# The last chunk's second product as 26 block products (4x4 by 4x2) in place of 28 (two times 2x2 by 2x2)

## The chip, the core and the metric

The kernel runs on one core of one Trainium2 chip. The metric is the device time of one launch in microseconds. Before the change it is 485.75 us, the median of 3 runs (485.72 to 485.87). The profile is of one execution, whose span is 485.1 us at a granted TensorE clock of 1.00; times "at 451.78" are microseconds from the start of that span.

## What is computed

A gated linear attention with a matrix state (mLSTM) is followed by a feed-forward block. Only the second is touched by the change:

```python
# x: (3072, 320), w_in: (320, 2048), w_out: (2048, 320), all float32
h = x @ w_in
g = h * (1.0 / (1.0 + np.exp(-1.702 * h)))
return (g @ w_out).astype(np.float32)
```

The kernel takes the sequence of 768 steps in six chunks of 128 (`w` = 0 to 5, `NW` = 6), for 4 batches and 8 heads. A chunk gives 4 blocks of 128 tokens, one for each batch, so for a chunk the first product is (512 x 320) by (320 x 2048) and the second (512 x 2048) by (2048 x 320). While the second product of chunk `w` runs, the attention of chunk `w+1` is woven between its parts. Chunk 5 has no successor: behind its first product there is only its second product and the stores.

## The kernel before: the parts that matter

Both products of chunks 1 to 5 are done in float32 with Strassen's scheme in Winograd's form: a 2x2 by 2x2 product of blocks takes 7 block products instead of 8, and sums of blocks of both factors have to be made for it. The order of the instructions on each engine is the order of the program.

The first product, one call for each half of the 2048 columns (`j` = 0 and `j` = 4), each over four pairs of column tiles `k`:

```python
def up_fast(w, j, between=None):
    ...
    if j == 0:                       # sums of the tokens' side, on VectorE (L506 to L509)
        V.tensor_tensor(out=bt1, in0=b01, in1=b00, op=OP.subtract)
        ...
    if between:
        between()                    # chunks 1 to 4, j == 0: work for the next chunk
    ...
    product(chain, 0, a00, b00, True)    # L518, TensorE
    take(0, 0)                           # L523, ScalarE: copy from PSUM
    product(other, 0, a01, b10, True)
    product(chain, 0, as2, bt2)
    take(0, 1)
    product(other, 1, as4, b11)
    product(chain, 0, a10, b01)
    take(1, 1)
    product(chain, 1, as1, bt1)
    for k in js:
        add(k, 0, 1, chain, 1)           # L526, VectorE: g = PSUM + g
    for k in js:
        for i, p in enumerate((other, chain)):
            r = slice(i * 64, i * 64 + 64)
            T.matmul(p[k], w_in_x[r, k, :], x[r, 2, :], start=False, stop=True, skip_group_check=True)  # L546
    for k in js:
        add(k, 1, 1, chain, 1)
        add(k, 0, 0, other, 0)
        gelu(k, 0, 0)                    # L530, ScalarE
    product(chain, 0, a11, bt4)
    for k in js:
        gelu(k, 1, 0, chain[k][:, ts[0]])
    for k in js:
        add(k, 0, 1, other, 1)
        gelu(k, 0, 1)
    for k in js:
        gelu(k, 1, 1)
```

The matmul at L546 on `chain[k]` writes the bank that `add(k, 0, 1, chain, 1)` has to read first, so it waits for that addition.

The second product, one call for each pair of batches `c`; each of its 7 products is 8 matmuls with 128x128 stationary and 160 moving columns:

```python
def product(a, b, *adds):
    po = ps_m.tile([128, DH], FP, tag="m", name="p_out")          # DH = 160
    for f in range(NH):                                           # NH = 8
        T.matmul(po, a(f), b[:, f, :], start=(f == 0), stop=(f == NH - 1))    # L615
    for dst, x in adds:
        if x is None:
            V.tensor_copy(out=dst, in_=po)                        # L618
        else:
            V.tensor_tensor(out=dst, in0=x, in1=po, op=OP.add)    # L620
```

The sums of `w_out` that it needs (`t1`, `t2`, `t4`, and `w01` in place) are made once in chunks 0 and 1 on VectorE (`weight_sums`, L585). The sums of the hidden values (`hidden_sums`, L596) are made in each chunk on VectorE, partly between the halves of the first product, partly beside the second.

Of the kernel before, what the change touches and what calls it, by code (L numbers as in the profile page):

```python
# [8 lines left out]
FP = mybir.dt.float32  # L9
U32 = mybir.dt.uint32  # L10
BF = mybir.dt.bfloat16
AF = mybir.ActivationFunctionType
OP = mybir.AluOpType
# [9 lines left out]
L = 128  # L23
# [11 lines left out]
def kernel(  # L35
# [12 lines left out]
    nc = tc.nc  # L48
    B, H, S, D = q.shape
    BH = B * H  # L50
    DM = H * D
    DFF = moe_w_in.shape[1]
    NW = S // L
    NP = H // 2
    NF = DFF // 128
    D1 = D + 1
    DP = 64
    W = B * L
    NH = NF // 2
    DH = DM // 2  # L60
# [5 lines left out]
    work = ctx.enter_context(tc.tile_pool(name="work", bufs=2))  # L66
    gp = ctx.enter_context(tc.tile_pool(name="gp", bufs=NH))
    op = ctx.enter_context(tc.tile_pool(name="op", bufs=2))
    rows = ctx.enter_context(tc.tile_pool(name="rows", bufs=2, space=bass.MemoryType.DRAM))
    ps_a = ctx.enter_context(tc.tile_pool(name="ps_a", bufs=4, space=PSUM))  # L70
    ps_m = ctx.enter_context(tc.tile_pool(name="ps_m", bufs=2, space=PSUM))
    ps_x = ctx.enter_context(tc.tile_pool(name="ps_x", bufs=2, space=PSUM))
    ctx.enter_context(tc.manual_schedule())

    V, A, G, T = nc.vector, nc.scalar, nc.gpsimd, nc.tensor
# [8 lines left out]
    k_st = const.tile([L, BH, DP], FP, name="k_st")  # L84
# [502 lines left out]
    def hidden_sums(w, c, js, *what):  # L587

        for j in js:
            s1, s2, s4 = (total(i, c)[:, 2 * j:2 * j + 2, :] for i in range(3))  # L590
            h00, h10, h01, h11 = (gs[w, k * 4 + j][:, :, (2 * c + two) * L:(2 * c + two + 1) * L]
                                  for k in range(2) for two in range(2))
            for x in what:
                out_, in0, in1, f = {1: (s1, h10, h11, OP.add), 2: (s2, s1, h00, OP.subtract),
                                     3: (h10, h00, h10, OP.subtract), 4: (s4, h01, s2, OP.subtract)}[x]
                V.tensor_tensor(out=out_, in0=in0, in1=in1, op=f)  # L596
# [5 lines left out]
    def down_fast(w, c):  # L602
        o = [op.tile([128, DM], FP, tag="o", name="o_sb") for _ in range(2)]
        o00, o01, o10, o11 = (o[i][:, n * DH:(n + 1) * DH] for i in range(2) for n in range(2))

        def block(two, k):
            return lambda f: gs[w, k * 4 + f // 2][:, f % 2, (2 * c + two) * L:(2 * c + two + 1) * L]

        def summed(i):
            return lambda f: total(i, c)[:, f, :]  # L610

        def product(a, b, *adds):
            po = ps_m.tile([128, DH], FP, tag="m", name="p_out")
            for f in range(NH):
# [4 lines that stand above are left out]
                else:  # L619
                    V.tensor_tensor(out=dst, in0=x, in1=po, op=OP.add)  # L620

        last = w == NW - 1 and c == 1

        def store(two, cols=slice(0, DM)):
            b = 2 * c + two
            nc.sync.dma_start(out=out[b * S + w * L:b * S + (w + 1) * L, cols], in_=o[two][:, cols])

        def left_done():

            if last:  # L630
                store(0, slice(0, DH))

        return [lambda: product(block(0, 0), w00, (o00, None), (o01, None)),
                lambda: (product(block(0, 1), w10, (o00, o00)), left_done()),
                lambda: product(summed(1), t2, (o01, o01)),
                lambda: product(block(1, 0), w01, (o10, o01)),
                lambda: product(summed(0), t1, (o11, o10), (o01, o01)),
                lambda: (product(block(1, 1), t4, (o10, o10)), store(1)),
                lambda: (product(summed(2), w11, (o01, o01)), store(0, slice(DH if last else 0, DM)))]

    def attention(w):
        if w > 1:

            return [[(columns, w)], [(weights, w, 0), (weights, w, 1)],
                    [(scores, w, 0), (hidden_sums, w - 1, 1, range(4), 3), (scores, w, 1), (weights, w, 2),
                     (weights, w, 3)],
                    [(values, w, 0), (values, w, 1), (scores, w, 2), (scores, w, 3)] +  # L650
                    [(scale, w, b) for b in (0, 1) if w + 1 < NW],
                    [(seam, w, 0), (seam, w, 1), (last_values, w)], [(carry, w)] if w + 1 < NW else [],
                    [(seam, w, 2)], [(seam, w, 3)]]
        return [[(columns, w)], [(weights, w, 0), (weights, w, 1)], [(scores, w, 0), (scores, w, 1)],
                [(weights, w, 2), (gates_out, w), (values, w, 0, 1), (scale, w, 0), (scale, w, 1)],
                [(weights, w, 3), (scores, w, 2), (scores, w, 3)], [(seam, w, 0), (seam, w, 1)],
                [(last_values, w)], [(seam, w, 2), (seam, w, 3)], [(new_states, w), (carry, w)]]
# [96 lines left out]
    def next_keys():  # L754
# [3 lines left out]
        transposes(w + 1, 0)  # L758
        transposes(w + 1, 1)

    for w in range(NW):
        more = w + 1 < NW
        for j in range(NF // 2):
            if w == 0 and j == 0:
                for pair_ in range(2):
                    for i, g in enumerate(hidden_of(0, pair_)):
                        A.activation(out=g, in_=first[pair_][i], func=AF.Gelu_apprx_sigmoid)
                    if pair_ == 0:
                        weights_in(0)
            elif w == 0 and j % 2 == 0:  # L770
                weights_in(j // 2)
                up(j, j == 2)
            elif w and j % 4 == 0:
                up_fast(w, j, next_keys if more and j == 0 else None)
            if w == 0 and j == 0:
                load_blocks(1, 0)
                spread(1)
                load_blocks(1, 1)
            if w == 1 and j == 3:
                weight_sums(3)  # L780
            if more:
                if w and j == 0:
                    load(w + 1, "o")
                if j == 4:
                    load(w + 1, "v")
                    if w:
                        spread(w + 1)
                    else:
                        fetch(17)
                        load(1, "o")  # L790
                if j == (4 if w else 6):
                    load(w + 1, "k")
                if w and j == 3:
                    for b in range(2, 4):
                        transposes(w + 1, b)
            if w and j in (3, 7):
                hidden_sums(w, 0, (j // 4 * 2, j // 4 * 2 + 1), 1, 2)
                if j == 3:
                    hidden_sums(w, 0, (0, 1), 3, 4)
        side = attention(w + 1) if more else []  # L800
        if w == 0:

            blocks = [(lambda b=b, n=n: down(w, b, n)) for ns in ((0, 1), (2,), (3,)) for b in range(B) for n in ns]
            stops = (0, 1, 5, 6, 8, 10, 12, 14, 15)
        else:
            blocks = down_fast(w, 0) + down_fast(w, 1)
            stops = (0, 1, 2, 4, 8, 10, 11, 12)
        for i, block in enumerate(blocks):
            if w == 0:
                weights_in(4 + i)  # L810
                if i == 0:
                    load_gates(2)
                if i == 2:
                    for b in range(B):
                        transposes(1, b, slice(0, 1))
                    first_sums((0, 1))
                    for b in range(B):
                        transposes(1, b, slice(1, 2))
                if i == 10:
                    load_blocks(2)  # L820
            elif w + 2 < NW and i == 0:
                load_gates(w + 2)
                load_blocks(w + 2)
            block()
            if i in stops and side:
                run(side.pop(0))
            if w == 1 and i == 1:
                weight_sums(2)
            if w:
                for at, c, *what in ((0, 0, (2, 3), 3), (1, 0, (2, 3), 4), (1, 1, range(4), 1),  # L830
                                     (5, 1, range(2), 2), (6, 1, range(2, 4), 2), (7, 1, range(4), 4)):
                    if i == at:
                        hidden_sums(w, c, *what)
                if i == 2 and not more:
                    hidden_sums(w, 1, range(4), 3)
            elif i == 11:
                weight_sums(0)
                weight_sums(1)
# [30 lines left out]
```

## Time and profile before

| what | value |
|---|---|
| device time, median of 3 | 485.75 us |
| span of the profiled run | 485.1 us |
| last chunk, first product, first half | 419.69 to 435.65 us |
| last chunk, first product, second half | 435.65 to 451.78 us |
| last chunk, second product (112 matmuls of the program) | 451.78 to 482.22 us |
| last addition and last store | 482.25 to 485.1 us |

The second product stands with x224 in the profile, because a float32 matmul of the program leaves two records there. The records' lengths overlap, so the mean of 301 ns beside L615 is not what one costs; the time from the start of one group to the start of the next is. The same holds on VectorE and GpSimd: an operation's duration includes the end of its pipeline, and the next one starts some 0.04 to 0.08 us before that end.

### The profile page before, as it was taken

How to read it: one execution, taken by the hardware profiler on the slowest of the kernel's cores; microseconds unless marked ns; L12 is line 12 of the kernel's file. 1: busy time of each engine (PE TensorE's matmuls, PEld its weight loads, DVE VectorE, ACT ScalarE, POOL GpSimd, SP SyncE). 2: the span in 40 equal slices, each digit the busy share in tenths (PEclk: the TensorE clock that was granted, in tenths of full speed). 3: DMA queues.
4: the chain of work that ended last, by engine and by line, in shares of the span. 5: the costliest groups of instructions: out<-in, count | busy, mean ns of one | idle time of the engine just before them, and what ended most of it. 6: DMA issues, size and time to landing. Idle time of an engine off the chain costs nothing. (4 is left out here: it accounts for less than half of the span.)

```text
span 485.1 us, 10434 instructions
## 1 busy us (share of the span) xinstructions
PE 479.3 (99%) x4072; PEld 397.8 (82%) x4072; DVE 343.0 (71%) x853; ACT 220.6 (45%) x575; POOL 60.4 (12%) x101
## 2 busy tenths in 40 slices
PE   8999999999999999999999999999999999999997
PEld 5874466777779999787999877999977999977997
DVE  8788887987978965667766677696576786254831
ACT  6767672603549302467600465900374920255300
POOL 3020001430000430000331000332000120000000
PEclk9999999999999999999999999999999999999999
DMA  9999689964996100997000896300492000000000
GB/s 126 197 262 286 112 208 191 170 85 71 153 215 73 14 28 30 188 178 82 4 29 9 122 249 70 32 28 3 79 262 26 1 15 16 28 1 0 1 34 22
DMA packets 176098, 44.87 MB, mean 92 GB/s; under 512 B 164369, under 2 KB 169649, under 8 KB 176049
## 3 DMA queue, kind: packets, MB, share of 16 engines
q1 hardware_dynamic: 175472, 43.55, 49.1%
q8 instruction: 32, 0.52, 0.4%
q10 hardware_dynamic: 576, 0.66, 0.4%
q14 instruction: 18, 0.14, 0.1%
HBM read 40.17 MB, written 4.01 MB: 91 GB/s over the span
## 5 line engine op out<-in xcount | busy, mean ns | idle before, releaser
L615 PE MATMUL p_out<-w_out_sb,g 128*128 128x160 f32 x480 | 69.8, 301 | 0.0
L615 PEld LDWEIGHTS p_out<-w_out_sb,g 128*128 128x128 f32 x480 | 66.3, 190 | 0.9
L405 ACT COPY xT<-p_x 128x384 f32<-128x384 f32 x24 | 10.8, 482 | 120.5 <-PE p_x L404 107.3
L526 DVE TENSOR_TENSOR g<-p_u,g 128x256 f32<-128x256 f32 x80 | 33.7, 424 | 44.6 <-PE p_u L518 35.0
L523 ACT COPY g<-p_u 128x256 f32<-128x256 f32 x120 | 43.0, 376 | 43.5 <-PE p_u L518 39.3
L530 ACT ACTIVATE g<-g 128x256 f32<-128x256 f32 x120 | 42.3, 423 | 39.3 <-DVE g L526 39.3
L336 POOL TENSOR_SCALAR_AFFINE_SELECT wt<-wt 128x1024 f32<-128x1024 f32 x20 | 22.7, 1136 | 240.9 <-ACT wt L334 201.9
L620 DVE TENSOR_TENSOR o_sb<-o_sb,p_out 128x160 f32<-128x160 f32 x70 | 21.4, 317 | 42.2 <-PE p_out L615 41.8
L334 ACT ACTIVATE wt<-wt,cols 128x128 f32<-128x128 f32 x160 | 47.9, 394 | 0.0
L518 PE MATMUL p_u<-xT,w_in_sb 128*128 128x256 f32 x160 | 38.9, 382 | 0.0
L518 PE MATMUL p_u<-xs,big 128*128 128x256 f32 x160 | 37.8, 379 | 0.0
L546 PE MATMUL p_u<-xT,w_in_x 64*128 64x512 f32 x80 | 37.0, 602 | 0.0
L546 PE MATMUL p_v<-xT,w_in_x 64*128 64x512 f32 x80 | 37.0, 602 | 0.0
L566 PE MATMUL p_out<-w_out_sb,g 128*128 128x320 f32 x128 | 36.4, 437 | 0.0
L352 DVE TENSOR_TENSOR wt<-p_s,wt 128x512 f32<-128x512 f32 x48 | 30.4, 682 | 8.2 <-POOL wt L336 6.7
L615 PE MATMUL p_out<-t,big 128*128 128x160 f32 x240 | 35.5, 301 | 0.0
L518 PEld LDWEIGHTS p_u<-xT,w_in_sb 128*128 128x128 f32 x160 | 29.6, 190 | 5.4 <-DVE o_sb L620 1.5
L518 PEld LDWEIGHTS p_u<-xs,big 128*128 128x128 f32 x160 | 30.0, 190 | 4.6
L615 PEld LDWEIGHTS p_out<-t,big 128*128 128x128 f32 x240 | 33.3, 190 | 0.2
L566 PEld LDWEIGHTS p_out<-w_out_sb,g 128*128 128x128 f32 x128 | 23.7, 190 | 10.0 <-issue 0.5
L526 DVE TENSOR_TENSOR g<-p_v,g 128x256 f32<-128x256 f32 x80 | 29.8, 414 | 0.0
L546 PEld LDWEIGHTS p_v<-xT,w_in_x 64*128 64x128 f32 x80 | 14.2, 186 | 16.0 <-issue 16.0
(172 smaller groups left out, 859.8 us busy)
## 6 DMA issues: line engine op xcount, KB each, us to landing
wt<-m_row SPq DMA_DIRECT2D x20, 512.0 KB, 6.9
v_st<-in_v_dram SPq DMA_DIRECT2D x5, 640.0 KB, 8.8
eo<-in_o_gate_dram SPq DMA_DIRECT2D x5, 640.0 KB, 5.6
k_st<-in_k_dram SPq DMA_DIRECT2D x5, 640.0 KB, 11.4
out_dram<-o_sb SPq DMA_DIRECT2D x19, 160.0 KB, 1.8
big<-in_moe_w_in_dram SPq DMA_DIRECT2D x5, 512.0 KB, 7.1
k_bl<-in_k_dram SPq DMA_DIRECT2D x40, 64.0 KB, 2.9
q_bl<-in_q_dram SPq DMA_DIRECT2D x40, 64.0 KB, 2.8
```

The lines of the kernel that those rows point to most:

```text
L334: A.activation(out=x[:, h, :], in_=x[:, h, :], func=AF.Exp, scale=-1.0, bias=cols[w][:, b * H + h:b * H + h + 1])
L336: G.affine_select(out=x, in_=x, compare_op=OP.is_ge, fill=0.0, base=0, pattern=[[0, H], [1, L]], channel_multiplier=-1)
L352: V.tensor_tensor(out=wt[w, b][:, :, i, :], in0=pw[i], in1=wt[w, b][:, :, i, :], op=OP.mult)
L405: A.copy(out=xT[w][:, :, b, :], in_=px)
L518: T.matmul(p[k][:, ts[t]], a[:, k // 2, k % 2 * 128:(k % 2 + 1) * 128], b, start=first, stop=True, skip_group_check=True)
L523: A.copy(out=g[k][i][:, ts[t]], in_=chain[k][:, ts[0]])
L526: V.tensor_tensor(out=g[k][i][:, ts[t]], in0=p[k][:, ts[pt]], in1=g[k][i][:, ts[t]], op=OP.add)
L530: A.activation(out=dst, in_=dst if src is None else src, func=AF.Gelu_apprx_sigmoid)
L546: T.matmul(p[k], w_in_x[r, k, :], x[r, 2, :], start=False, stop=True, skip_group_check=True)
L566: T.matmul(po, gs[w, f // 2][:, f % 2, b * L:(b + 1) * L], w_out_sb[:, f, :], start=(f == 0), stop=(f == NF - 1))
L615: T.matmul(po, a(f), b[:, f, :], start=(f == 0), stop=(f == NH - 1))
L620: V.tensor_tensor(out=dst, in0=x, in1=po, op=OP.add)
```

## The change: what it does and what it is for

In the last chunk the second product is no longer cut into two 2x2 by 2x2 products, which take 7 + 7 products of eight matmuls, or 28 when they are counted in products of four matmuls. It is taken as one product of a 4x4 grid of blocks (4 batches by 4 quarters of the 2048) by a 4x2 grid (4 quarters by 2 halves of the 320 columns). A scheme with 26 products of four matmuls does this, where the plain way has 32. For it,

- 21 operations on 128x640 blocks of `w_out` make its sums of weights: 8 on VectorE and 13 on GpSimd, written in program order behind the four sums of tokens (L506 to L509), in the first half of the first product (`last_weights`, as `between` of `j == 0`). They use memory that attention no longer needs;
- the sums of the hidden values, `a_form`, are made on VectorE: eight (`a_early`, 15 operations) ahead of the additions of the second half of the first product (as `between` of `j == 4`), three (`a_next`) and 21 (`a_late`) among the products;
- the results of products that have the same bank number in `steps` are summed in PSUM; 35 additions or copies take them into the four output tiles, 30 on VectorE and 5 on ScalarE.

In chunk 5 `hidden_sums` falls away. Chunks 0 to 4 are as they were. The core of the diff:

```diff
+    def last_weights():
+        ...                      # names of rooms and of the blocks b[k, n] of w_out
+        form(V, 16, b[2, 0], b[0, 0], sub)
+        form(V, 6, b[0, 0], b[3, 0], sub)
+        form(V, 8, b[1, 0], b[3, 0], sub)
+        form(V, 1, b[1, 0], wf[16], sub)
+        form(V, 18, b[1, 1], t3[0], sub)
+        form(V, 9, b[1, 1], wf[16], sub)
+        form(V, 17, b[1, 0], b[2, 0], add)
+        form(V, 2, wf[18], b[3, 1], sub)
+        form(G, 23, b[3, 1], t3[1], sub)
+        form(G, 4, wf[18], b[1, 1], add)
+        form(G, 4, wf[4], wf[23], sub)
+        form(G, 7, b[1, 1], b[3, 1], sub)
+        ...                      # nine more on G: 26, 10, 20, 12, 13, 11, 15, 14, 22
+    def a_form(name, x, y, f, neg=False):
+        ...                      # two V.tensor_tensor of 128x256, or one of 128x512
+    a_early = [(9, (1, 0), (3, 1), ADD), (17, (2, 1), (3, 1), ADD), (16, (2, 0), (3, 1), ADD),
+               ("d", (1, 0), (1, 1), SUB), (24, "d", 17, ADD), (26, (3, 1), "d", SUB), (26, (0, 1), 26, ADD),
+               (25, 17, (2, 0), SUB)]
+    a_next = [(21, (0, 0), (0, 1), ADD), (19, (0, 0), (3, 0), ADD), (18, (2, 0), (3, 0), ADD)]
+    a_late = [(10, (1, 0), (1, 2), ADD), (20, 10, 17, SUB), (12, (1, 0), (3, 2), SUB), ...]
+    def down_last():
+        ...
+        steps = [(6, None, (0, 0), "+00 -30"), (8, None, (0, 1), "+00 -10"), (1, 6, (3, 1), "-10 +30"),
+                 (4, 4, (1, 0), "-31"), (9, 5, None, "+10"), (17, 1, None, "+20"), ...,
+                 (23, 4, None, "+21"), (22, 2, None, "-01"), (25, 6, None, "-20")]
+        for i, (n, chain, block, takers) in enumerate(steps):
+            if i < 3:
+                a_form(*a_next[i])
+            else:
+                for _ in range(2 if i in (4, 6, 8, 10) else 1):
+                    if late:
+                        a_form(*late.pop(0))
+            p, first = bank(chain)
+            for f in range(4):
+                a = a_block(*block, f // 2)[:, f % 2, :] if block else af[n][:, f, :]
+                T.matmul(p, a, wf[n][:, f, :], start=(first and f == 0), stop=(f == 3), skip_group_check=True)
+            for taker in takers.split():
+                ...              # V.tensor_tensor or, for a tile's first value, V.tensor_scalar or A.activation
+            if n in stores:
+                ...              # five stores, the last of 128x160
-                up_fast(w, j, next_keys if more and j == 0 else None)
+                up_fast(w, j, (next_keys if j == 0 else None) if more else last_weights if j == 0 else early_sums)
-            if w and j in (3, 7):
+            if more and w and j in (3, 7):
                 hidden_sums(w, 0, (j // 4 * 2, j // 4 * 2 + 1), 1, 2)
+        if not more:
+            down_last()
+            break
-                if i == 2 and not more:
-                    hidden_sums(w, 1, range(4), 3)
```

In the order that the changed kernel has on VectorE, the eight weight sums stand behind L509 and ahead of all additions (L526) of the first half; the 15 operations of `a_early` stand behind the additions of the first half and ahead of those of the second.

## The prediction, written before the changed kernel was run

> **What bounds the kernel now.** I read the page first, then the chain that ended last in order of time, then the busy time in stretches, and at the end the timeline around two places.
>
> From the page, the busy times of the engines:
>
> ```profile
> PE 479.3 (99%) x4072; PEld 397.8 (82%) x4072; DVE 343.0 (71%) x853; ACT 220.6 (45%) x575; POOL 60.4 (12%) x101
> ```
>
> TensorE (PE) is busy for 99% of the span. Busy is not the same as needed, so the chain (start, length, what) has to confirm it for the last chunk:
>
> ```profile
> 437.58 1.73 PE p_v L518 x8
> 439.31 1.74 PE p_u L518 x8
> 441.04 1.73 PE p_v L518 x8
> 442.77 3.45 PE p_u L518 x16
> 446.22 0.62 PE p_v L546
> ...
> 451.78 30.44 PE p_out L615 x224
> 482.22 0.02 issue
> 482.25 0.32 DVE o_sb L620
> ```
>
> From 419.69 to 482.22 the chain is TensorE without a hole. The second product is one piece of 30.44 us; behind it stand one addition (0.32 us) and a store, to 485.1. So each matmul taken out counts in full, as long as nothing else holds TensorE. The stretches (length, then busy time of PE, PEld, DVE, ACT, POOL) show who has room:
>
> ```profile
> 420.00:430.00 10.00, 10.00 (x47) 8.66 (x46) 2.42 (x8) 5.47 (x13) 0.00 (x0) 1.00 0.05 17
> 435.00:440.00 5.00, 5.00 (x24) 4.28 (x24) 3.94 (x12) 5.00 (x18) 0.00 (x0) 1.00 0.00 0
> 440.00:445.00 5.00, 5.00 (x25) 4.39 (x24) 0.03 (x1) 2.76 (x8) 0.00 (x0) 1.00 0.00 0
> 475.00:480.00 5.00, 5.00 (x39) 5.00 (x38) 0.87 (x3) 0.00 (x0) 0.00 (x0) 1.00 0.01 3
> ```
>
> VectorE (DVE) has 7.6 free us of ten in the first stretch and nearly all of the third; GpSimd (POOL) does nothing here. This is the room that the change means to fill.
>
> **What the Trainium skill says.** "SBUF — State Buffer", section "Who interferes with whom": a VectorE instruction with two SBUF inputs and a GpSimd instruction that reads SBUF share a port and exclude each other; the second one waits until the first is through. One with a single SBUF input (the other in PSUM) does not contend. The trace of before agrees, twice:
>
> ```profile
> 154.34 1.10 POOL L336 TENSOR_SCALAR_AFFINE_SELECT wt<-wt 128x1024 f32<-128x1024 f32 x1 [38.97 <-DMA q_bl<-in_q_dram]
> 154.41 1.31 DVE L596 TENSOR_TENSOR xs<-g 128x256 f32<-128x256 f32 x1
> ...
> 244.11 0.74 POOL L411 TENSOR_TENSOR v_st<-v_st,cols 128x328 f32<-128x328 f32 x1
> ...
> 243.70 2.47 DVE L352 TENSOR_TENSOR wt<-p_s,wt 128x512 f32<-128x512 f32 x4
> ```
>
> A hidden sum that takes 0.42 us elsewhere took 1.31 us, because it arrived 0.07 us behind a GpSimd operation of 1.10 us. The additions with one input in PSUM ran beside GpSimd with no delay (2.47 us for four, 0.60 each).
> "GPSIMD Engine Reference", section "Elementwise — side-by-side cycle accounting", gives some 2.6 cycles an element for a two-input operation on GpSimd. At its 1.2 GHz this is an estimate of 1.39 us for 640 elements. The trace has 328 elements only (0.735 us, 0.695 from start to start).
> "Perfetto Trace Analysis", section "Identifying the Most-Contended Engine": weight-load time says more of TensorE's limit than matmul time. Here PEld is 5.00 of 5.00 in the second product, so TensorE is really full there.
>
> **The change part by part.**
>
> *Removed from TensorE.* 30.44 us / 112 matmuls = 0.272 us for one of 128x160. The new product has 26 x 4 = 104 of the same shape: 104 x 0.272 = 28.27 us. Gain: 8 x 0.272 = **2.17 us**, 0.45% of the time. This is the most that the change can bring; the end (an addition, a store of the same 80 KB) stays.
>
> *Weight sums on VectorE.* L585 takes 1.41 us from start to start for 1280 elements (102.83 to 104.24), and 256 elements take 0.34, so 640 take 0.74. Eight take 5.9 us. They start behind L509, at 421.43, and would end at 427.35; the first addition of this half starts at 429.04. Alone they would be free.
>
> *Weight sums on GpSimd.* A copy of 64 elements takes 0.244 us, nearly all of it fixed. With 0.19 us fixed, the 0.735 us of 328 elements leave 1.66 ns an element, so 640 take 1.25 us, or 1.21 from start to start. By plain proportion they take 0.695 x 640/328 = 1.36. I work with 1.21 and keep 1.36 for the range. The first of the 13 (number 23) can go at 412. The second needs VectorE's fifth sum (18), at 421.43 + 5 x 0.74 = 425.13 and some 0.15 of pipeline and semaphore. From there both engines want the port and, I assume, alternate: VectorE to 425.9, GpSimd to 427.1, VectorE to 427.8, GpSimd to 429.0, VectorE's last to 429.75. So the additions start at 429.75 instead of 429.04. TensorE needs the first of them by 430.3, so it loses 0 to 0.2 us here. The additions read PSUM and take no port. GpSimd's other ten run from 429.75.
>
> *Early hidden sums.* 14 operations of 256 elements (0.34) and one of 512 (0.61) are 5.4 us. The first reads block (3, 1), whose last four gelus are the end of this half's ScalarE work (eight from 436.17 in 2.56 us). So they can't start ahead of 438.1. Alone they would end at 443.6, ahead of the additions at 444.97. But four of GpSimd's ten are not done at 438.1: the seventh ends at 429.75 + 7 x 1.21 = 438.2. Alternating, three VectorE and three GpSimd operations take 3 x (0.34 + 1.21) = 4.65, to 442.85; the other 12 take 4.45, to 447.3. A little luck in who comes first takes half a microsecond off. The additions of the second half stand behind, in program order. These lines of before (the timeline) show how much slack they have:
>
> ```profile
> 444.97 1.72 DVE L526 TENSOR_TENSOR g<-p_u,g 128x256 f32<-128x256 f32 x4 [5.96 <-PE p_u L518]
> ...
> 446.16 0.18 PEld L546 LDWEIGHTS p_u<-xT,w_in_x 64*128 64x128 f32 x1
> ```
>
> The first addition (0.42) has to be done by 446.16, so it may start at 445.7. It will start at 446.8 to 447.3: TensorE stands for **1.1 to 1.6 us**, and I take 1.3. With 1.36 us for a GpSimd operation the same ledger gives 448.6 and 2.9 us; with 1.1 us it gives nearly nothing.
>
> *Second product.* VectorE: 6 + 28 operations of 256 elements (0.34) are 11.6 us, 7 of 512 (0.61) are 4.3, and 30 takers of 160 (two take 0.55, of which the second adds 0.24) are 7.2. Sum 23.0 us beside 28.3 of TensorE. The densest part, steps 3 to 10, has 12 sums (8.1) and 6 takers (1.4), 9.5 us against 8.7, but these sums are used many steps later. I expect no wait, or 0.1. GpSimd's sums end at 443 to 445, ahead of the product.
>
> Sum: 485.75 - 2.17 + 0.1 + 1.3 + 0.1 = 485.1, and I say **485.0 us**.
>
> **The rivals.** First, *the sums stay hidden* and TensorE gains all: 483.6. For it: VectorE's free time, and that a tuned kernel's sums were presumably placed by trial. Against it: the port; 13 operations of 1.2 us or more leave nearly no free port from 425 to 443. Second, *the port holds the first product harder*: 1.36 us or more for a GpSimd operation, or GpSimd keeping the port through several. Then TensorE stands for 2.9 to 3.5 us and the time is 486.5 to 487.3. For it: plain proportion and the skill's cycles. Third, *VectorE becomes the bound of the second product*: if each operation costs 15% more than I read, 26.5 of 28.3 us are filled, and takers that come late hold the PSUM banks of products two steps later. I give this 1 to 2 us and one chance in six. Fourth, *the weight sums come too late for the products*; they'd have to be 7 us later than by my ledger.
>
> **Range and chances.** The low end is the pure gain with a little less of something else: 483.5. The high end is the second rival with a little of the third: 487.4. Nothing that I can find moves the time by 9.7 us, which is 2%.
>
> **What would show it.** In the chain, the second product is one piece of 28.3 us (x208); a longer one speaks for the third rival. TensorE's hole in the second half of the first product, ahead of L546 and waiting for VectorE's L526, is 1.1 to 1.6 us; there is little or none in the first half. GpSimd's sums read 1.25 us where VectorE is not in their way and up to 0.4 more beside it; VectorE's 256-element sums at 438 to 443 read 1.3 to 1.6 instead of 0.42. I am wrong if the port goes to VectorE's row of sums as a whole (then no hole), if GpSimd's sums last over 1.3 us, or if the second product has holes of its own.

## The result, and the profile after

The changed kernel takes **490.72 us** (median of 6 runs, 489.9 to 495.56) against 485.82 us (median of 6) before: a ratio of 1.0112, 95% interval 1.0071 to 1.0153. The prediction said 485.0 us and at most 487.4. The profiled execution has a span of 488.1 us. In it the last chunk begins 1.15 us earlier than in the profile of before (418.54 instead of 419.69). That lead comes from the first chunk, which the change does not touch: the profiled execution of before took 486.87 us, 1.1 us more than the median. So times of after are moved by 1.15 us where they are compared with those of before. The profiled execution of after is the fastest of its six (489.9 us).

The chain that ended last, in order of time (start, length, what), around the second half of the first product:

```profile
437.00 0.02 issue
437.02 9.41 DVE kT L719 x8
446.43 0.03 issue
446.45 2.70 DVE qT L719 x7
449.15 0.34 DVE g L526
449.50 0.04 issue
449.54 0.69 PE p_u L546
...
451.44 0.84 PE p_u L546
452.28 0.01 PE p_v L546
452.29 0.84 PE p_u L546
...
456.86 28.34 PE p_out L769 x208
485.20 0.03 issue
485.22 0.32 DVE u L774
```

Three things can be read here. The second product is one piece of 28.34 us (it was 30.44), so the 8 matmuls saved give 2.10 us. Ahead of it the chain leaves TensorE: it runs through the early hidden sums (L719) on VectorE, of which the first eight take 9.41 us, and through the first addition (L526), to the 64-row matmul (L546), which starts at 449.54. In what follows, the "hole" is this wait of TensorE. And the pairs of 64-row matmuls come every 0.84 us, where they came every 0.43 before.

The stretches show the third point (columns: length; busy time of PE, PEld, DVE, ACT, POOL; the granted TensorE clock; DMA):

```profile
446.00:448.00 2.00, 0.14 (x1) 0.00 (x0) 1.97 (x6) 0.00 (x0) 0.00 (x0) 1.00 0.00 0
448.00:450.00 2.00, 0.46 (x2) 0.30 (x4) 2.00 (x7) 0.00 (x0) 0.00 (x0) 1.00 0.00 0
450.00:451.00 1.00, 1.00 (x6) 0.41 (x4) 0.78 (x3) 0.00 (x0) 0.00 (x0) 0.82 0.00 0
451.00:452.00 1.00, 1.00 (x4) 0.35 (x2) 0.46 (x2) 0.42 (x1) 0.00 (x0) 0.50 0.00 0
452.00:453.00 1.00, 1.00 (x6) 0.42 (x3) 0.68 (x2) 0.00 (x0) 0.00 (x0) 0.50 0.00 0
453.00:454.00 1.00, 1.00 (x5) 0.48 (x2) 0.07 (x1) 0.42 (x1) 0.00 (x0) 0.50 0.00 0
454.00:455.00 1.00, 1.00 (x3) 0.24 (x3) 0.78 (x3) 0.19 (x1) 0.00 (x0) 0.98 0.00 0
```

TensorE stands while VectorE is full, and later its clock is at 0.50 for some 3.4 us. How long it stands is read from TensorE's timeline:

```profile
445.01 1.12 PE L546 MATMUL p_v<-xT,w_in_x 64*128 64x512 f32 x2
449.54 0.69 PE L546 MATMUL p_u<-xT,w_in_x 64*128 64x512 f32 x1 [3.40 <-DVE g L526]
```

The first 64-row matmul writes the other bank (`p_v`) and runs in time, so TensorE is idle for 3.40 us, from 446.14. What makes VectorE so slow is seen when the timeline is cut to single operations (start, length, engine, line, what):

```profile
436.85 1.54 POOL L665 TENSOR_TENSOR eo<-t,w_out_sb 128x640 f32<-128x640 f32 x1
438.35 1.72 POOL L665 TENSOR_TENSOR wt<-w_out_sb 128x640 f32<-128x640 f32 x1
...
437.02 1.65 DVE L719 TENSOR_TENSOR kT<-g 128x256 f32<-128x256 f32 x1 [2.08 <-ACT g L530]
438.60 1.76 DVE L719 TENSOR_TENSOR kT<-g 128x256 f32<-128x256 f32 x1
440.28 1.76 DVE L719 TENSOR_TENSOR kT<-g 128x256 f32<-128x256 f32 x1
441.96 1.76 DVE L719 TENSOR_TENSOR kT<-g 128x256 f32<-128x256 f32 x1
443.65 1.76 DVE L719 TENSOR_TENSOR kT<-g 128x256 f32<-128x256 f32 x1
445.33 0.41 DVE L719 TENSOR_TENSOR kT<-g 128x256 f32<-128x256 f32 x1
```

As long as GpSimd has sums left, one VectorE sum comes for each of them, every 1.68 us, and GpSimd's own take 1.72 instead of 1.54. When GpSimd ends, at 445.1, the next one takes 0.41 us.

The account, against the reordered kernel below, which has no hole (its times moved by -0.07 us): the 64-row matmuls that wait begin 449.54 - 445.08 = **4.46 us** late; the second product begins 456.86 - 450.63 = **6.23 us** late, so another **1.77 us** are lost, 1.7 of them at the halved clock (with two sums ahead, below, where the profile shows the full clock, the same stretch loses 0.08); 2.10 are gained. 6.23 - 2.10 = 4.1 us; with the lead of 1.15 us taken off, that is the 3.0 us between the two spans.

### The profile page after: what moved, and what is told of

Read it like the earlier page. It is cut to its first block, busy times and chain, and to the rows that moved or that the text cites. A ratio compares the mean times of both kernels' runs of the same rounds, so it can differ in the third digit from the quotient of the medians.

```text
span 488.1 us, 10478 instructions
## 1 busy us (share of the span) xinstructions
PE 479.3 (98%) x4056; PEld 396.4 (81%) x4056; DVE 367.2 (75%) x897; ACT 222.3 (46%) x580; POOL 82.5 (17%) x114
## 5 line engine op out<-in xcount | busy, mean ns | idle before, releaser
L526 DVE TENSOR_TENSOR g<-p_u,g 128x256 f32<-128x256 f32 x80 | 33.4, 423 | 34.0 <-PE p_u L518 23.2
L615 PE MATMUL p_out<-w_out_sb,g 128*128 128x160 f32 x384 | 56.1, 301 | 0.0
L615 PEld LDWEIGHTS p_out<-w_out_sb,g 128*128 128x128 f32 x384 | 53.1, 190 | 0.9
L546 PE MATMUL p_u<-xT,w_in_x 64*128 64x512 f32 x80 | 38.7, 625 | 3.4 <-DVE g L526 3.4
L546 PE MATMUL p_v<-xT,w_in_x 64*128 64x512 f32 x80 | 38.8, 625 | 0.0
L620 DVE TENSOR_TENSOR o_sb<-o_sb,p_out 128x160 f32<-128x160 f32 x56 | 17.0, 316 | 26.9 <-PE p_out L615 26.5
L566 PEld LDWEIGHTS p_out<-w_out_sb,g 128*128 128x128 f32 x128 | 23.8, 190 | 9.8 <-issue 0.5
L526 DVE TENSOR_TENSOR g<-p_v,g 128x256 f32<-128x256 f32 x80 | 29.8, 414 | 0.0
L615 PE MATMUL p_out<-t,big 128*128 128x160 f32 x192 | 28.5, 301 | 0.0
L615 PEld LDWEIGHTS p_out<-t,big 128*128 128x128 f32 x192 | 26.6, 190 | 0.2
L350 PE MATMUL p_s<-qT,kT 40*128 40x128 f32 x384 | 26.0, 280 | 0.4 <-ACT wt L330 0.4
```

What stands on the lines that cost most here:

```text
L350: T.matmul(pw[i][:, p, :], kT[w, b][r, p, :], qT[w, b][r, p, :], start=True, stop=True)
L526: V.tensor_tensor(out=g[k][i][:, ts[t]], in0=p[k][:, ts[pt]], in1=g[k][i][:, ts[t]], op=OP.add)
L566: T.matmul(po, gs[w, f // 2][:, f % 2, b * L:(b + 1) * L], w_out_sb[:, f, :], start=(f == 0), stop=(f == NF - 1))
```

## The experiments

**Theory A**: GpSimd's weight sums and VectorE's early sums exclude each other, the additions wait behind the early sums, TensorE behind the additions. **Theory B**: VectorE simply has too much of its own work there. **Theory C**, beside A: part of the loss is the clock.

**GpSimd's sums left out.** This kernel leaves out the 13 sums; the products take plain blocks of weights in their place.

```diff
         def form(E, name, x, y, f):
+            if E is G:
+                wf.setdefault(name, x)
+                return
```

> The 13 weight sums on GpSimd are left out (the products take a plain block of the weights instead), all else stays, VectorE's work too. Theory A (the shared port: early hidden sums wait behind GpSimd's sums, the additions behind them, and TensorE behind those): no hole ahead of the second half's 64-row matmuls, eight early sums of 256 elements in 2.8 us instead of 9.4, clock 1.00 throughout, time 483.6 (483.2 to 484.2). Theory B (VectorE has too much of its own work there, GpSimd or not): the hole stays at 3 us or more and the time at 488 to 491.

Measured: 483.91 us, ratio 0.9964 (0.9950 to 0.9977). VectorE's sums are the same in number and place, but they now take (timeline):

```profile
439.04 2.44 DVE L722 TENSOR_TENSOR kT<-g 128x256 f32<-128x256 f32 x7 [0.18 <-ACT g L530]
```

Seven in 2.44 us, 0.34 each from start to start; TensorE has no hole and the clock is 1.00. B falls: with the same work on VectorE the loss is gone.

**Early sums left out.** This kernel leaves out the eight early hidden sums and writes their tiles with memsets.

```diff
+            if skip:
+                V.memset(af[name], 0.0)
+        if skip:
+            return
         ...                      # early_sums calls a_form with skip=True
```

> The eight early hidden sums (15 operations) are left out; seven memsets stand in their place, so that the tiles are written. GpSimd's sums stay. Theory A: GpSimd alone holds nothing up, because the additions read PSUM: no hole, GpSimd's sums 1.54 us each throughout, time 483.3 to 484.2. Theory B says the same of the hole, for VectorE has less to do. A third reading (GpSimd slows the additions themselves or ScalarE): a hole of over 1 us stays and the time is over 486.

Measured: 483.86 us, ratio 0.9964 (0.9952 to 0.9976), no hole. GpSimd's sums run through to 444.5, 1.54 to 1.56 us each where they do not wait, and TensorE does not notice. So neither row of sums alone does harm; the two together do. What they share is, by the prediction, the port; no run here tells a port from another shared path.

**TensorE kept busy in the hole.** Nothing is left out; twenty matmuls with zeros are added to a bank.

```diff
+        if w == NW - 1 and j:
+            for _ in range(20):
+                T.matmul(other[js[0]], idle, idle.unsqueeze(1).to_broadcast([128, 4, 128]), start=False, stop=True,
+                         skip_group_check=True)
```

> Twenty matmuls with zeros (4.3 us) are added to a PSUM bank ahead of the second half's 64-row matmuls, where TensorE stands otherwise. They add nothing to the result. Theory C (part of the loss is TensorE's halved clock behind the hole, 1.75 us in the profiled run): clock 1.00 there, the 64-row matmuls take 3.6 us instead of 5.4, time 488.2 to 489.0, and the spread of the runs (489.9 to 495.6) shrinks to under 1 us. Rival (the additions set the pace there, and the clock costs nothing): time stays at 490 to 491.

Measured: 488.13 us (488.05 to 488.57), ratio 1.0049 (1.0035 to 1.0063). The chain:

```profile
445.53 4.32 PE p_v L545 x20
449.85 0.62 PE p_v L550
450.47 0.23 PE p_u L550
450.70 0.20 PE p_v L550
```

The additions come as late as before, and the wait is only filled; but the pairs of 64-row matmuls come every 0.43 us again, and the runs lie within some 0.5 us of each other. The clock, not the wait, was worth 490.72 - 488.13 = 2.6 us in the median. Theory C holds beside A. The wait without the clock accounts for the rest: 485.82 - 2.10 + 4.46 = 488.2.

Why 2.6 in the median and 1.7 in the profile? The six runs of the change have mean clocks of 0.996 to 0.997 (489.9 to 490.07 us), 0.993 (491.37 and 491.63) and 0.986 (495.56). Taken as time at half clock this is, as an estimate, 3 to 4, 7 and 14 us, or one, two and four stretches of 3.4 us. Only the fastest of them has a trace; where the others lost their clock is not shown. The trace of the last experiment below, with 0.993, has one stretch of 6.8 us at 0.50 that begins in its hole.

**The same sums in another order on GpSimd.** In the changed kernel GpSimd's second sum (number 4) waits 11.4 us for VectorE's fifth, while others that need nothing of VectorE stand behind it. Here four of these go ahead of it, so that five stand before the wait instead of one.

```diff
         form(G, 23, b[3, 1], t3[1], sub)
-        form(G, 4, wf[18], b[1, 1], add)
-        form(G, 4, wf[4], wf[23], sub)
         form(G, 7, b[1, 1], b[3, 1], sub)
         form(G, 26, b[1, 0], b[1, 1], sub)
+        form(G, 11, b[3, 0], t3[1], sub)
+        form(G, 14, b[1, 1], b[3, 0], sub)
+        form(G, 4, wf[18], b[1, 1], add)
+        form(G, 4, wf[4], wf[23], sub)
         ...                      # the other six
```

> Nothing is left out: the same 13 sums on GpSimd in another order, five that need nothing of VectorE first (at 411 to 419, where GpSimd waited 11.4 us before), eight behind VectorE's fifth sum. GpSimd would end at about 438 instead of 445. Theory A: the early sums have the port for themselves, hole under 0.3 us, clock 1.00, time 483.6 (483.3 to 484.3), under the kernel before by 0.3 to 0.5%. Theory B: order on GpSimd changes nothing, 490 to 491. If GpSimd's first five hold up the four sums of tokens at 419, a hole of 1 to 2 us appears in the first half instead.

Measured: **483.80 us** (483.70 to 484.76), ratio 0.9961 (0.9949 to 0.9974). It computes all that the reference asks for and is faster than both kernels. Its timeline and chain:

```profile
435.30 3.04 POOL L665 TENSOR_TENSOR t<-w_out_sb 128x640 f32<-128x640 f32 x2
...
437.08 3.89 DVE L719 TENSOR_TENSOR kT<-g 128x256 f32<-128x256 f32 x8 [2.08 <-ACT g L530]
...
443.89 1.72 DVE L526 TENSOR_TENSOR g<-p_u,g 128x256 f32<-128x256 f32 x4 [0.18 <-PE p_u L518]
```

```profile
445.15 0.62 PE p_v L546
...
450.70 28.34 PE p_out L769 x208
479.04 0.02 issue
479.06 0.32 DVE u L774
```

GpSimd ends at 438.3, the eight early sums take 3.89 us (1.3 of them the wait for its last one), and the additions wait for TensorE again, with 0.18 us to spare.

**Three and two sums ahead** in place of one or five, to see whether the hole follows the ledger, and from which length on the clock is lost. The edit is the same, with 23, 7, 26 or 23, 7 ahead of number 4.

> The same sums, with three on GpSimd ahead of the wait for VectorE's fifth sum (one in the changed kernel, five in the reordered one). The ledger with 1.50 us from start to start: seven of the ten behind the wait are done when the early sums begin, two more come between them, the additions start 1.9 us too late. Hole 1.6 to 2.2 us. If a hole of this length leaves the clock alone, the time is 485.4 to 486.1; if any hole halves it, 487 or more. If the hole did not depend on how many GpSimd sums are left over: 490.

> The same with two ahead. Three GpSimd sums come between the early sums: the additions start 3.3 us too late, hole 3.0 to 3.6 us. Without any loss of clock the time is 486.9 to 487.4; with the halved clock of the changed kernel, 488.5 to 489.5 and a spread of a microsecond or more.

| GpSimd sums ahead | waiting 64-row matmuls late | TensorE idle in the profile | median time | mean clock of the runs |
|---|---|---|---|---|
| 5 | 0 | 0 | 483.80 us | 0.999 to 1.0 |
| 3 | 1.67 us | 0.6 us | 485.58 us | 0.999 to 1.0 |
| 2 | 3.14 us | 2.1 us | 487.0 us | nine runs 0.999 to 1.0, six 0.996 |
| 1 (the change) | 4.46 us | 3.4 us | 490.72 us | 0.986 to 0.997 |

The idle time with three and with two ahead, from TensorE's waits (us in total, times, longest):

```profile
PE p_u L546 <- DVE g L526: 0.6, 1, 0.6
...
PE p_u L546 <- DVE g L526: 2.1, 1, 2.1
```

The ratios are 0.9992 (0.9983 to 1.0001) with three ahead and 1.0036 (1.0026 to 1.0045) with two. With three ahead nothing is clearly won against before: 1.7 us of waiting eat the 2.1 saved. With two ahead the 15 runs fall in two groups: nine with the full clock at 486.8 to 487.4 us, six with 0.996 at 488.3 to 488.8. The step between the groups is the same 1.7 us that the profile of the change shows. I had expected one or the other, not both. The one profile is of a run with the full clock; that the six lost theirs behind this hole is inferred from the mean clock and the step.

**What an operation costs on GpSimd.** Three operations more, their results overwritten later.

```diff
+        G.tensor_tensor(out=room[:, 0:328], in0=flat[:, 0:328], in1=flat[:, 640:968], op=OP.add)
+        G.tensor_tensor(out=room[:, 0:640].rearrange("p (a b) -> p a b", b=40),
+                        in0=flat[:, 0:640].rearrange("p (a b) -> p a b", b=40), in1=few, op=OP.mult)
+        G.tensor_tensor(out=room[:, 640:1280], in0=flat[:, 0:640], in1=flat[:, 640:1280], op=OP.add)
```

> Three more operations on GpSimd in the time in which it waits for VectorE's fifth sum (411 to 424), their results overwritten later: a plain sum of 328 elements, a product of 640 elements with a second operand that repeats each value 40 times (the form of the scaling of values, from whose 0.735 us the prediction took its cost), and a plain sum of 640. If the repeated operand made the row of the prediction too cheap: plain 328 takes 0.85 to 0.90 us, repeated 640 1.25 to 1.35, plain 640 1.54. If the cost is one line in the number of elements whatever the operand: 0.735, 1.54, 1.54. The time of the kernel stays at 489.5 to 492.

```profile
424.17 2.87 POOL L681 TENSOR_TENSOR k_bl<-w_out_sb 128x328 f32<-128x328 f32 x1 [11.43 <-DVE w_out_sb L665]
427.12 1.26 POOL L682 TENSOR_TENSOR k_bl<-w_out_sb 128x640 f32<-128x640 f32 x1
428.33 1.54 POOL L684 TENSOR_TENSOR k_bl<-w_out_sb 128x640 f32<-128x640 f32 x1
```

640 elements take 1.54 us plain and 1.26 us when the second operand repeats each value 40 times. (The sum of 328 stood 1.98 us at the port, as the first sum behind VectorE's fifth does in every run: 3.52 - 1.54. That leaves 0.89.) The row from which the prediction took its cost was of the cheaper kind. I had overlooked that the added operations read the block that VectorE's fifth sum writes, so they waited for it too and pushed GpSimd's row back by some 3.7 us: one run, 492.99 us, above the expected range.

## Why the prediction was wrong, step by step

- *Removed from TensorE*, 2.17 us: right. The piece is 28.34 us where 28.27 were reckoned.
- *Weight sums on VectorE*, 0.74 us each: right (0.73 to 0.74). That they would alternate with GpSimd was wrong: VectorE made its last three in a row while GpSimd stood for 1.98 us. So the additions of the first half were not late at all, and GpSimd began later than reckoned.
- *Weight sums on GpSimd*: **the step that failed.** I took 1.21 us from start to start; they take 1.50. Over the 12 sums behind the wait that is 12 x 0.29 = 3.5 us. With 1.50 in place of 1.21, the prediction's ledger starts the last ten sums at 430.4, has four of them left when the sixth ends at 439.4, and the early sums done at about 450.7: a wait of about 5.0 us, or 4.5 with the half microsecond taken off that the prediction allowed itself. It had said 1.3; 4.46 were measured. Its own sign ("I am wrong [...] if GpSimd's sums last over 1.3 us") came true. The Trainium skill's 2.6 cycles an element ("GPSIMD Engine Reference", "Elementwise — side-by-side cycle accounting"), from which I had 1.39 us, were the better guide, though 0.15 us under the 1.54 measured. I preferred a row of this trace, and it had a repeated operand.
- *Early sums* behind the port, with the additions behind them: right in kind, shown by leaving out either row. They alternate one by one, as assumed, at 1.68 us a pair; each GpSimd sum costs VectorE 1.34 us of waiting. (The ledger's last twelve sums come to 4.35 us, not 4.45; this moves nothing.)
- *The sum* left out a term: such a hole can cost TensorE its clock, 1.7 us in the profiled run and 2.6 in the median. The Trainium skill has this in "TensorE: Matmul & The Clock Gate", "What's actually happening": the clock is halved after an idle window of some 3.4 us, and the windows run on their own, whenever the work begins. The runs agree in part: the halved stretch of the profile lasts 3.4 us (450.64 to 454.05), and the same program loses it in some runs and not in others. They don't agree that TensorE must be idle for a whole window: in the 3.4 us before the clock falls it had been at work again for 1.1, and with 2.1 us of idle time 6 of 15 runs lost clock (0 of 12 with 0.6, 6 of 6 with 3.4). How little work is enough to keep the clock was not tried.
- *Second product*: no holes, as predicted; VectorE was busy for 23.27 of 28.20 us in it (23.0 reckoned). The third rival did not happen.
- *The rivals*: the second one (a harder hold of the port, 486.5 to 487.3) was the right one, but even without the loss of clock it did not go far enough: 488.13 us with TensorE kept busy. The first (483.6) is what the reordered kernel reached, 483.80.

So the idea of the change was sound and its gain was real; an order on GpSimd that put a waiting sum in front of ready ones turned 2.1 us of gain into 4.9 us of loss.

## What to carry to other kernels

An engine that looks idle is not free room when it shares a port with the engine that feeds the bound: look for two-input SBUF operations of both in the same stretch, and order the helper's queue so that what can run early does. Take an operation's cost from a row of the same operand form, not only of the same engine and operation. Where TensorE may stand idle for 2 us or more, as in the row with two sums ahead, reckon with its clock as well, and look at the spread of the runs: two groups 1.7 us apart were the sign here.

## What the runs showed of the hardware that I had not expected

- A GpSimd product with a repeated second operand costs 1.26 us for 640 elements, a plain sum 1.54.
- Who gets the shared port was not the same in both places: three VectorE sums in a row at 424 (GpSimd stood for 1.98 us), strictly one by one at 438 to 445 (1.68 us a pair). What decides it was not tried and stays open.
- One and the same program, with TensorE idle for 2.1 us in its profile, kept the full mean clock in 9 of 15 runs and showed 0.996 in 6; matmuls with zeros in the longer hole of the change held it in all four runs.
